# Attention, MoE and top-2 MoE on one core: the float64 weights are converted by VectorE alone, with an integer addition, under a new hand-written order

## The chip, the cores and the metric

The kernel runs on one core of a Trainium2 chip. A core has TensorE (PE, matrix products, with PEld for its weight loads), VectorE (DVE), ScalarE (ACT), GpSimd (POOL) and SyncE (SP, which issues most DMA transfers here). Each engine takes its own queue in order, and semaphores make one wait for another. The metric is the device time of the whole program in microseconds. Runs of this kernel differ by about 0.5% (1080.51 to 1086.46 us).

## The reference

```python
# q, k, v, f_logit: (4, 8, 768, 48) float32
f = 1 / (1 + exp(-f_logit))
for t in range(768):                      # decaying linear attention, state per head 48 x 48
    state = f[t][:, None] * state + outer(k[t], v[t])
    y[t] = q[t] @ state
x = y as (3072 tokens, 384)
x = relu(x @ w_in) ** 2 @ w_out           # 384 -> 2048 -> 384; w_in and w_out are float64
noisy = x @ w_gate + log1p(exp(x @ w_noise)) * noise       # 8 experts, the two largest per token
out = sum over the two: share * (relu(x @ w1[e]) @ w2[e])  # 384 -> 1024 -> 384
```

## The kernel before

**Stages.** Attention works in 24 chunks of 128 tokens, all 8 heads at once. Chunk by chunk there are preparation steps (f, k and q transposed and multiplied by products of decays, which VectorE makes with two scans) and attention units (`a_A`, `a_k`, `a_U`, `a_Y` twice with `a_S`). Three chunks make a block of 384 tokens. The first MoE goes over 8 blocks and 16 slices of its inner width, 128 units in all: `mm1` (9 products), ScalarE's relu and square, VectorE's low part `gl`, and two units later `mm2` (9 products). Then come the choice of experts, the gathering of rows by GpSimd, and the second MoE.

**High and low parts.** TensorE's operands are pairs: a high part rounded to the engine's fast type and a low part, the rest. Three products (high by high, high by low, low by high) make one exact enough product. So every weight piece needs a high and a low part.

**The weights of the first MoE.** They come as float64 words in 16 pieces (`w_load`, alternately of `w_in` and `w_out`, each 128 partitions by 768 numbers of two 32-bit words). The first four have staging places of their own, the others share one place for each kind, so the load of a piece waits until the piece two before it has been read. `conv_a` builds the float32 number from the high word, with sign, exponent and 20 bits of the mantissa: on VectorE a shift (line 379), a step that sets the sign (line 380) and a mask that keeps the exponent (`cv_p`, line 382). ScalarE turns the low word into a float (line 387; VectorE does it for pieces 0, 12 and 14 with a product, line 385) and rounds the high part (line 390). GpSimd multiplies the low word's float by the exponent (line 392) and joins the two (line 393). `conv_b` subtracts the high part to get the low part (line 403): on GpSimd, and on VectorE for pieces 8 and 15 (`BY_DVE`).

**Other work on the same engines.** On VectorE: the scans (lines 472, 482), a limit on four numbers between them (line 474, `rF`), the masked products `AM` (515), the state (`S`, 532 and 533), the low parts of x (589), the square `g` for units 8 to 31 (625) and `gl` (628). On GpSimd: the products of q from chunk 6 on (494).

**The order.** Up to the end of the second pass over the weights (units 0 to 31) the order of the program is written out in a string, `ORDER`: W and E, V are loads, P preparation steps, a attention units, A and B the two halves of a conversion, x the low parts of attention's result, M units of the first MoE, L the opening of a pool. Each event appends its instructions to the engines' queues, SP's DMA queue among them. Behind it a loop issues unit after unit, with fixed offsets for all else.

Of the kernel before, what the change touches and what calls it, by code (L numbers as in the profile page):

```python
# [24 lines left out]
def general_path(tc, psum, dram, ident, wide, q, k, v, f_logit, w_in_v, w_out_v, w_gate, w_noise, noise, w1, w2, out,  # L25
                 rt):
    """The same function for any input, token after token, then tile after tile over all experts."""
# [150 lines left out]
def kernel(  # L178
# [52 lines left out]
    # ---------------------------------------------------------------- pools of the first phase  # L231
# [9 lines left out]
    # ---------------------------------------------------------------- constants  # L241
# [40 lines left out]
    # what the scans over the decays of all pairs add: they start anew in the columns between two pairs  # L282
# [24 lines left out]
    # ---------------------------------------------------------------- weights of the first MoE  # L307
# [23 lines left out]
    def w_load(i):  # L331
        """Rows of w_in come in the order of the rows of x^T."""
        kind, p = ("in", "out")[i % 2], i // 2
        n = 256 * WORDS
        shape = [128, 3, n] if kind == "in" else [128, 2, DM * WORDS]
        if i < RING:
            st = wpool.tile(shape, WDT, tag="w", name="st_first")
        else:
            st = LP["p"].tile(shape, WDT, tag=f"st_{kind}", name=f"st_{kind}", bufs=1)
        if kind == "in":  # L340
            for (r0, m, row0, rs) in ((0, 48, 0, 96), (64, 48, 48, 96), (48, 16, 288, 16), (112, 16, 336, 16)):
                s = bass.AP(tensor=w_in_v.tensor, offset=w_in_v.offset + row0 * DFF * WORDS + p * n,
                            ap=[[DFF * WORDS, m], [rs * DFF * WORDS, 3], [1, n]])
                nc.sync.dma_start(st[r0:r0 + m], s)
        else:
            nc.sync.dma_start(st, w_out_v[p * 256:p * 256 + 256, :].rearrange("(a p) d -> p a d", p=128))
        stage[i] = st

    CV = {}

    def w_parts(i):
        """The places of a piece in the tiles of high and low parts."""
# [9 lines left out]
        # columns in the order that the 32x32 transposes of r_store undo  # L362
# [7 lines left out]
    def conv_a(i):  # L370
        """float64 words to the nearest float32: the high word holds sign, exponent and 20 bits of
        the mantissa, the low word the rest. Signs and exponents come out right for magnitudes in
        [2**-126, 2); others raise the flag."""
        st = stage.pop(i)
        if wide:
            src = st.rearrange("p a (f w) -> p (a f) w", w=2)
            lo_w, hi_w = src[:, :, 0], src[:, :, 1]
            a = LP["p"].tile([128, 768], I32, tag="cv_a", name="cv_a", bufs=2)
            nc.vector.tensor_scalar(a, hi_w, 0x08000000, 3, op0=OP.bitwise_xor, op1=OP.logical_shift_left)
            nc.vector.scalar_tensor_tensor(a, hi_w, -2147483648, a, op0=OP.bitwise_and, op1=OP.bitwise_xor)  # L380
            e = LP["p"].tile([128, 768], I32, tag="cv_p", name="cv_p", bufs=1)
            nc.vector.tensor_scalar(e, a, -8388608, None, op0=OP.bitwise_and)
            x = mp.tile([128, 768], F32, tag=f"x2{'ab'[i % 2]}", name="cv_x", bufs=1)
            if i in (0, 12, 14):
                nc.vector.scalar_tensor_tensor(x, lo_w.bitcast(U32), -2.0 ** -52, e.bitcast(F32), op0=OP.mult, op1=OP.mult)
            else:
                nc.scalar.activation(x, lo_w.bitcast(U32), AF.Copy, scale=-2.0 ** -52)
            a_f = a.bitcast(F32)
            for h_, _, cut in w_parts(i):
                nc.scalar.activation(h_, cut(a_f), AF.Copy, scale=-1.0)  # L390
            if i not in (0, 12, 14):
                nc.gpsimd.tensor_tensor(x, x, e.bitcast(F32), op=OP.mult)
            nc.gpsimd.tensor_tensor(x, x, a_f, op=OP.subtract)
        else:
            x = st.rearrange("p a f -> p (a f)")
            for h_, _, cut in w_parts(i):
                nc.scalar.activation(h_, cut(x), AF.Copy)
        CV[i] = x

    def conv_b(i, eng):  # L400
        x = CV.pop(i)
        for h_, l_, cut in w_parts(i):
            eng.tensor_tensor(l_, cut(x), h_.bitcast(F32), op=OP.subtract)

    # ---------------------------------------------------------------- attention
# [99 lines left out]
    def a_A(c):  # L505
        # the two heads of a pair lie in different rows of the array and run at the same time
# [37 lines left out]
    def a_Y(c, h):  # L544
# [5 lines left out]
        for p in (2 * h, 2 * h + 1):  # L550
            for s in range(2):
                # 16 rows more than the head has: they make room for a part of the last pair.
                # Only a half's first product clears the bank: the others find their columns cleared
# [31 lines left out]
    def a_x(c):  # L585
# [5 lines left out]
        if i == BT - 1:  # L591
            # the last pair's rows go where the other pairs leave room
# [5 lines left out]
    # ---------------------------------------------------------------- first MoE  # L598
    GB, acc = {}, {}

    # the first block is cut in two around the second, which gives the conversion of the weights time
# [62 lines left out]
    # ---------------------------------------------------------------- routing  # L664
# [15 lines left out]
    def r_logits(j):  # L680
        """The three parts of the sum over the model's width side by side in the array's columns."""
# [15 lines left out]
    def exp_a(x, n, w, names):  # L697
        """exp(x) of values that are not above zero, as the quotient of two sigmoids."""
# [25 lines left out]
    def softplus_noise(lg, pos, en, ln, noi_, n):  # L724
        """The logits with noise times softplus(x) = max(x, 0) + log1p(exp(-|x|))."""
# [110 lines left out]
    # ---------------------------------------------------------------- second MoE  # L836
# [12 lines left out]
    def segments(name, src, n, ne):  # L849
        """Rows in quarters: 32 partitions take one quarter each of 32 tokens."""  # L850
# [28 lines left out]
    def whole(e, t):  # L879
        """The first tokens are in a hurry: whole rows, and the tensor engine transposes them."""  # L880
# [9 lines left out]
    def gather_T(e, t):  # L890
        """x^T in the order of rows of the first MoE's x2^T: 32x32 blocks of the quarters are transposed."""
# [47 lines left out]
    # the first two experts take turns, which gives the last tokens' choices time  # L939
# [28 lines left out]
    def emm2(U):  # L968
# [5 lines left out]
        if final(e, hf):  # L974
            # tile after tile: only the last one's rows are still to be added when the products end
# [13 lines left out]
        if flipped(e, hf):  # L989
            # y^T: no columns for slots that are not there  # L990
# [55 lines left out]
    # ---------------------------------------------------------------- is the fast path exact?  # L1046
# [27 lines left out]
    def judge(step):  # L1074
        """Out of the fast path's reach: a weight's magnitude, a decay over a chunk that is too
        small to be divided by, or more tokens of an expert than its share of slots."""
# [25 lines left out]
    # ---------------------------------------------------------------- program  # L1102
# [3 lines left out]
    # The order of events up to the end of the second pass over the weights of the first MoE: loads (W) and  # L1106
    # conversion (A, B) of weights, loads of rows (E, V), preparation (P) and products (a, x) of attention,
    # products with the weights (M)
    ORDER = """
    P0 P1 P2 E1 W0 V0 P3 V1 P4 P5 P6 P7 a0 a1 P8 E2 W1 A0 E3 B0 a2 P9 W2 W3 P10 V2 a3 E4 P11 a4 V3 P12  # L1110
    A1 x0 a5 P13 a6 a7 P14 B1 W4 P15 A2 W5 a8 P16 B2 a9 A3 a10 E5 x1 W6 P17 V4 P18 a11 B3 P19 a12 a13 A4
    P20 a14 V5 P21 x2 W7 P22 B4 W8 a15 P23 a16 A5 a17 P24 a18 P25 A6 a19 B5 V6 P26 a20 P27 P28 M0 a21 M1
    P29 a22 B6 P30 a23 A7 x3 a24 W9 A8 W10 P31 x4 a25 P32 a26 M2 a27 M3 V7 W11 B7 P33 a28 a29 A9 x5 B8
    W12 M4 A10 P34 W13 P35 B9 W14 a30 M5 M6 V8 B10 a31 P36 M7 A11 a32 W15 A12 M8 B11 M9 a33 P37 M10 A13
    M11 B12 M12 B13 A14 P38 M13 A15 L0 a34 B14 M14 P39 M15 P40 a35 M16 a36 M17 x6 a37 P41 a38 a39 B15
    P42 M18 M19 a40 M20 P43 a41 M21 P44 a42 V9 a43 a44 P45 M22 x7 M23 P46 x8 P47 a45 M24 M25 P48 V10 M26
    a46 M27 a47 P49 a48 M28 P50 M29 M30 M31 V11
    """
    # pieces whose second half DVE converts
    BY_DVE = (8, 15)  # L1120
    # loads of v and steps of preparation that are among them
# [109 lines left out]
    uE = (NBLK - 1) * NF + LAG - 1  # L1231
    at(uE + 6, snapshot)
# [5 lines left out]
    def expert(n, loads, splits, gathers, flips):  # L1238
        """When the weights of an expert are loaded and split, and its tokens gathered and transposed."""
# [23 lines left out]
    def open_late():  # L1263
        """Where the weights were converted is room for another block of x."""
# [15 lines left out]
    def first_block(u):  # L1280
# [8 lines left out]
        "W": w_load, "A": conv_a, "B": lambda i: conv_b(i, nc.vector if i in BY_DVE else nc.gpsimd),  # L1289
# [7 lines left out]
    for u in range(2 * NF, NU + NEU + LAG):  # L1297
        if u == (NBLK - 1) * NF:
            open_p2()
        # first product  # L1300
# [8 lines left out]
        # attention runs ahead  # L1309
# [3 lines left out]
        # second product  # L1313
# [13 lines left out]
    # ---------------------------------------------------------------- the general path  # L1327
# [33 lines left out]
```

## Time and profile before

| | |
|---|---|
| median of 3 runs | 1085.11 us (1080.51 to 1086.46) |
| span of the profiled execution, first to last instruction | 1078.5 us |
| what lies around the span in that execution | not in the trace |
| TensorE busy | 1008.9 us (94%) |
| VectorE busy | 648.9 us (60%) |
| ScalarE busy | 492.9 us (46%) |
| GpSimd busy | 471.3 us (44%) |

Busy is the time in which an engine works on an instruction. Registers, branches, semaphores and the issue of DMAs don't count. Matmuls are pipelined, so a busy TensorE is not one at its peak.

### The profile page before, as it was taken

To read this page: it belongs to the slowest core of one execution; us is meant where nothing else is said; L and a number is where in the kernel's file an instruction comes from. 1 tells how busy PE (TensorE), PEld (TensorE's weight loads), DVE (VectorE), ACT (ScalarE), POOL (GpSimd) and SP (SyncE) were. 2 spreads that over 40 slices of the span, in tenths; PEclk is the share of its full clock that TensorE was granted. 3 is DMA by queue.
4 is the path that set the end of the run, shared out by engine and by line. 5 is a ranking of instruction groups with operands and counts; after the bars stand their busy time and mean duration, and the time that the engine had idled before them with its cause. 6 is when DMAs were issued, how large, how long until landed. Compare 5 with 4: busy or idle time off the path is not lost. (4 is left out here: it accounts for less than half of the span.)

```text
span 1078.5 us, 17435 instructions
## 1 busy us (share of the span) xinstructions
PE 1008.9 (94%) x6381; PEld 929.8 (86%) x6381; DVE 648.9 (60%) x1298; ACT 492.9 (46%) x1024; POOL 471.3 (44%) x527
## 2 busy tenths in 40 slices
PE   6577789999999999999999898999999999999996
PEld 4456779999889899898999787999989899999996
DVE  7999988878778777685335673353443443434420
ACT  2334434465556555555656642353343444434321
POOL 3775661003200303113123547777575757575523
PEclk9688889999999999999999999999999999999999
DMA  9886535547573645441023625344443535363413
GB/s 178 169 151 142 120 89 143 150 107 166 131 190 102 166 113 116 130 106 48 1 65 97 143 64 100 57 115 99 100 104 80 105 80 125 69 141 66 100 20 48
DMA packets 144782, 115.80 MB, mean 107 GB/s; under 512 B 75888, under 2 KB 128112, under 8 KB 144688
## 3 DMA queue, kind: packets, MB, share of 16 engines
q1 hardware_dynamic: 127248, 90.94, 35.6%
q0 software_dynamic: 15488, 20.52, 11.7%
q10 hardware_dynamic: 1952, 3.15, 1.2%
q8 instruction: 52, 0.85, 0.3%
q14 instruction: 42, 0.34, 0.1%
HBM read 89.08 MB, written 23.11 MB: 104 GB/s over the span
## 5 line engine op out<-in xcount | busy, mean ns | idle before, releaser
L875 POOL DMA_INDIRECT gr<-x2s,seg x192 | 186.7, 972 | 74.4 <-issue 47.2
L615 PE MATMUL mm<-x,inh 128*128 128x384 f32 x768 | 203.2, 346 | 9.4 <-ACT r L618 9.4
L963 DVE SCALAR_TENSOR_TENSOR hl<-mm,hh 128x512 fp32r<-128x512 f32 (+1 forms) x120 | 71.6, 597 | 167.2 <-ACT hh L962 167.0
L615 PEld LDWEIGHTS mm<-x,inh 128*128 128x128 f32 x768 | 139.6, 192 | 14.0 <-ACT r L618 10.5
L628 DVE TENSOR_TENSOR gl<-g,gh 128x384 fp32r<-128x384 f32 x128 | 82.2, 646 | 106.1 <-ACT gh L623 85.6
L953 PE MATMUL mm<-gxh,eh 128*128 128x320 f32 (+1 forms) x384 | 138.1, 360 | 8.4 <-DVE hl L963 7.0
L1039 POOL DMA_INDIRECT out_dram<-y,tt x56 | 92.6, 1653 | 104.4 <-ACT y L1037 93.8
L648 PE MATMUL a<-gh,outh 128*128 128x384 f32 x384 | 136.5, 355 | 0.2
L953 PE MATMUL mm<-gxl,eh 128*128 128x320 f32 (+1 forms) x384 | 136.2, 355 | 0.4 <-DVE gxl L909 0.4
L953 PE MATMUL mm<-gxh,el 128*128 128x320 f32 (+1 forms) x384 | 135.9, 354 | 0.0
L962 ACT ACTIVATE hh<-mm 128x512 fp32r<-128x512 f32 (+1 forms) x120 | 62.4, 520 | 154.3 <-PE mm L953 153.8
L648 PE MATMUL a<-gl,outh 128*128 128x384 f32 x384 | 130.2, 339 | 1.5 <-DVE gl L628 1.5
L615 PE MATMUL mm<-x,inl 128*128 128x384 f32 x384 | 131.0, 341 | 0.0
L648 PE MATMUL a<-gh,outl 128*128 128x384 f32 x384 | 130.0, 338 | 0.0
L494 POOL TENSOR_TENSOR qT<-qT,F 128x512 f32<-128x512 f32 x18 | 24.5, 1361 | 228.9 <-DVE qT L418 179.9
L618 ACT ACTIVATE r<-mm 128x384 f32<-128x384 f32 x128 | 62.0, 484 | 81.1 <-PE mm L615 79.5
L953 PEld LDWEIGHTS mm<-gxh,eh 128*128 128x128 f32 x384 | 72.5, 189 | 16.2 <-DVE hl L963 8.7
L318 DVE TENSOR_TENSOR el<-est,eh 128x512 fp32r<-128x512 f32 x96 | 64.5, 686 | 36.1 <-ACT eh L315 35.8
L953 PEld LDWEIGHTS mm<-gxh,el 128*128 128x128 f32 x384 | 72.6, 189 | 8.8
L953 PEld LDWEIGHTS mm<-gxl,eh 128*128 128x128 f32 x384 | 72.6, 189 | 6.7 <-DVE gxl L909 0.7
L648 PEld LDWEIGHTS a<-gh,outh 128*128 128x128 f32 x384 | 73.0, 190 | 5.9 <-issue 2.6
L648 PEld LDWEIGHTS a<-gl,outh 128*128 128x128 f32 x384 | 73.1, 190 | 2.3 <-DVE gl L628 2.2
(242 smaller groups left out, 2180.3 us busy)
## 6 DMA issues: line engine op xcount, KB each, us to landing
est<-in_moe_w_dram SPq DMA_DIRECT2D x56, 192.0 KB, 4.4
est<-in_moe_w_dram SPq DMA_DIRECT2D x14, 768.0 KB, 5.6
ck<-in_moe_w_in_dram SPq DMA_DIRECT2D x8, 768.0 KB, 5.2
ck<-in_moe_w_out_dram SPq DMA_DIRECT2D x8, 768.0 KB, 5.1
out_dram<-zeros SPq DMA_DIRECT2D x46, 128.0 KB, 3.4
v<-in_v_dram SPq DMA_DIRECT2D x24, 192.0 KB, 5.1
st_out<-in_moe_w_out_dram SPq DMA_DIRECT2D x6, 768.0 KB, 5.1
x2s<-x2q SPq DMA_DIRECT2D x32, 144.0 KB, 2.5
```

What stands on the lines that cost most here:

```text
L318: nc.vector.tensor_sub(lo, x, hi.bitcast(F32))
L494: eng.tensor_tensor(qT[c], PT.pop((c, "q")) if c < EARLY else qT[c], F, op=OP.mult)
L615: nc.tensor.matmul(ph, a[:, c, fs], b_[:, c, :], start=(n == 0), stop=(n == 8))
L618: nc.scalar.activation(r, ph, AF.Relu)
L628: nc.vector.tensor_sub(gl, g, gh.bitcast(F32))
L648: nc.tensor.matmul(acc[j][d], a[:, f % 4, ds_], b_, start=(first and n == 0), stop=(last and n == 2))
L875: nc.gpsimd.indirect_dma_start(out=g[:, b, :], out_offset=None, in_=src, in_offset=bass.IndirectOffsetOnAxis(ap=idx, axis=0))
L953: nc.tensor.matmul(ph[:, :n], a[:, c, fs], b_[:, c, o:o + n], start=(i == 0), stop=(i == 8))
L962: nc.scalar.activation(hh[:, :n], ph[:, :n], AF.Relu)
L963: nc.vector.scalar_tensor_tensor(hl[:, :n], ph[:, :n], 0.0, hh[:, :n].bitcast(F32), op0=OP.max, op1=OP.subtract)
L1039: st = nc.gpsimd.indirect_dma_start(out=out, out_offset=bass.IndirectOffsetOnAxis(ap=slots(e, T)[:m, 0:1].bitcast(I32), axis=0), in_=y[:m] ...
```

## The change

`conv_a` no longer splits off the exponent and no longer uses GpSimd. ScalarE scales the unsigned low word by 2^-29 and writes it as an integer, a number from 0 to 8: the three bits that the shift leaves empty, rounded. VectorE makes the high word with its sign, as before with another constant, and adds the integer to the number's bits. ScalarE does this for all 16 pieces. The high part becomes an event of its own, H (`conv_h`). `conv_b` always runs on VectorE. `a` lies in the ring places that `cv_x` had, and `cv_u` takes the place of `cv_a` and `cv_p` in the conversion's pool.

The order of the first phase is new. It has the same events otherwise: 16 loads and conversions, 51 preparation steps, 49 attention units, 9 events x, 32 units M. One more thing moves: `snapshot`, a copy of the experts' counts, from unit `uE + 6` to `uE + 1` near the end of the first MoE, while `uE` itself has the same value. Everything else in the diff is comments.

```diff
         if wide:
             src = st.rearrange("p a (f w) -> p (a f) w", w=2)
             lo_w, hi_w = src[:, :, 0], src[:, :, 1]
-            a = LP["p"].tile([128, 768], I32, tag="cv_a", name="cv_a", bufs=2)
-            nc.vector.tensor_scalar(a, hi_w, 0x08000000, 3, op0=OP.bitwise_xor, op1=OP.logical_shift_left)
+            u = LP["p"].tile([128, 768], I32, tag="cv_u", name="cv_u", bufs=2)
+            nc.scalar.activation(u, lo_w.bitcast(U32), AF.Copy, scale=2.0 ** -29)
+            a = mp.tile([128, 768], I32, tag=f"x2{'ab'[i % 2]}", name="cv_a", bufs=1)
+            nc.vector.tensor_scalar(a, hi_w, 0x18000000, 3, op0=OP.bitwise_xor, op1=OP.logical_shift_left)
             nc.vector.scalar_tensor_tensor(a, hi_w, -2147483648, a, op0=OP.bitwise_and, op1=OP.bitwise_xor)
-            e = LP["p"].tile([128, 768], I32, tag="cv_p", name="cv_p", bufs=1)
-            nc.vector.tensor_scalar(e, a, -8388608, None, op0=OP.bitwise_and)
-            x = mp.tile([128, 768], F32, tag=f"x2{'ab'[i % 2]}", name="cv_x", bufs=1)
-            if i in (0, 12, 14):
-                nc.vector.scalar_tensor_tensor(x, lo_w.bitcast(U32), -2.0 ** -52, e.bitcast(F32), op0=OP.mult, op1=OP.mult)
-            else:
-                nc.scalar.activation(x, lo_w.bitcast(U32), AF.Copy, scale=-2.0 ** -52)
-            a_f = a.bitcast(F32)
-            for h_, _, cut in w_parts(i):
-                nc.scalar.activation(h_, cut(a_f), AF.Copy, scale=-1.0)
-            if i not in (0, 12, 14):
-                nc.gpsimd.tensor_tensor(x, x, e.bitcast(F32), op=OP.mult)
-            nc.gpsimd.tensor_tensor(x, x, a_f, op=OP.subtract)
+            nc.vector.tensor_tensor(a, a, u, op=OP.add)
+            CV[i] = a.bitcast(F32)
...
-    def conv_b(i, eng):
+    def conv_h(i):
+        for h_, _, cut in w_parts(i):
+            nc.scalar.activation(h_, cut(CV[i]), AF.Copy)
+
+    def conv_b(i):
         x = CV.pop(i)
         for h_, l_, cut in w_parts(i):
-            eng.tensor_tensor(l_, cut(x), h_.bitcast(F32), op=OP.subtract)
+            nc.vector.tensor_tensor(l_, cut(x), h_.bitcast(F32), op=OP.subtract)
...
     ORDER = """
-    P0 P1 P2 E1 W0 V0 P3 V1 P4 P5 P6 P7 a0 a1 P8 E2 W1 A0 E3 B0 a2 P9 W2 W3 P10 V2 a3 E4 P11 a4 V3 P12
-    A1 x0 a5 P13 a6 a7 P14 B1 W4 P15 A2 W5 a8 P16 B2 a9 A3 a10 E5 x1 W6 P17 V4 P18 a11 B3 P19 a12 a13 A4
-    P20 a14 V5 P21 x2 W7 P22 B4 W8 a15 P23 a16 A5 a17 P24 a18 P25 A6 a19 B5 V6 P26 a20 P27 P28 M0 a21 M1
...
+    E1 P0 P1 P2 P3 a0 P4 P5 P6 V0 W0 a1 A0 E2 P7 W1 A1 H0 W2 E3 P8 V1 a2 a3 a4 V2 W3 P9 x0 B0 P10 W4
+    H1 A2 a5 P11 W5 P12 a6 B1 P13 H2 P14 E4 a7 a8 P15 B2 a9 a10 x1 a11 A3 V3 P16 a12 W6 P17 a13 P18
+    a14 A4 E5 P19 V4 H3 P20 x2 a15 P21 W7 a16 H4 B3 P22 B4 W8 P23 P24 A5 P25 V5 a17 A6 H5 a18 P26 P27
+    P28 H6 a19 B5 a20 M0 x3 M1 A7 V6 M2 B6 A8 a21 H7 a22 P29 a23 a24 B7 P30 W9 a25 x4 W10 P31 P32 a26
+    P33 a27 H8 M3 P34 a28 A9 a29 W11 B8 x5 M4 V7 W12 W13 A10 M5 H9 H10 P35 a30 V8 a31 B9 M6 A11 M7 B10
+    a32 a33 W14 H11 M8 W15 M9 A12 P36 M10 H12 B11 A13 P37 M11 H13 B12 M12 B13 M13 M14 A14 A15 H14 L0
+    P38 a34 a35 M15 M16 P39 M17 P40 a36 M18 P41 a37 B14 x6 a38 a39 M19 a40 V9 x7 H15 B15 P42 a41 P43
+    M20 P44 M21 V10 a42 a43 P45 a44 M22 x8 M23 V11 M24 P46 P47 a45 M25 M26 P48 P49 M27 M28 a46 M29 P50
+    M30 a47 a48 M31
     """
-    BY_DVE = (8, 15)
...
-    uE = (NBLK - 1) * NF + LAG - 1
-    at(uE + 6, snapshot)
+    uE = (NBLK - 1) * NF + 1
+    at(uE + 1, snapshot)
...
-        "W": w_load, "A": conv_a, "B": lambda i: conv_b(i, nc.vector if i in BY_DVE else nc.gpsimd),
+        "W": w_load, "A": conv_a, "H": conv_h, "B": conv_b,
```

## Rows read from the trace of the kernel before

**Rows 1.** The page: busy time, share, instructions; TensorE's busy tenths in 40 slices.

```profile
PE 1008.9 (94%) x6381; PEld 929.8 (86%) x6381; DVE 648.9 (60%) x1298; ACT 492.9 (46%) x1024; POOL 471.3 (44%) x527
...
PE   6577789999999999999999898999999999999996
```

**Rows 2.** Busy time by stage: PE, PEld, DVE, ACT, POOL, clock, DMA, GB/s.

```profile
0.00:66.00 66.00, 40.41 (x310) 30.94 (x312) 58.11 (x75) 21.85 (x43) 38.46 (x58) 0.84 1.01 169
66.00:160.00 94.00, 71.80 (x436) 65.79 (x434) 86.72 (x93) 41.84 (x84) 59.41 (x36) 0.85 0.60 125
160.00:1078.00 918.00, 896.64 (x5647) 833.10 (x5643) 504.02 (x1132) 429.25 (x897) 373.47 (x435) 1.00 0.44 101
```

**Rows 3.** Waits from 0 to 160 us: in total, times, longest.

```profile
PE t L526 <- ACT cv_x L387: 9.2, 1, 9.2
...
PE t L554 <- DVE AM L515: 7.1, 1, 7.1
...
ACT y L583 <- PE t L558: 4.5, 1, 4.5
```

**Rows 4.** Busy time in two short stretches, columns as in rows 2.

```profile
6.00:12.00 6.00, 5.27 (x23) 3.46 (x23) 5.62 (x9) 1.01 (x3) 0.00 (x0) 1.00 1.30 180
12.00:18.00 6.00, 3.68 (x36) 2.92 (x32) 5.79 (x9) 1.10 (x2) 0.00 (x0) 1.00 1.39 165
```

**Rows 5.** VectorE's timeline there: start, duration in us, line, operation.

```profile
6.00 1.26 DVE L472 TENSOR_TENSOR_SCAN F<-fT,anew 128x528 f32<-128x528 f32 x1 [4.01 <-ACT fT L442]
7.29 0.17 DVE L474 TENSOR_SCALAR rF<-F 128x4 f32<-128x4 f32 x1
...
7.71 1.25 DVE L482 TENSOR_TENSOR_SCAN G<-fT,anew 128x524 f32<-128x524 f32 x1
...
15.92 0.55 DVE L379 TENSOR_SCALAR cv_a<-st_first 128x768 int32<-128x768 int32 x1
16.50 0.96 DVE L380 SCALAR_TENSOR_TENSOR cv_a<-st_first,cv_a 128x768 int32<-128x768 int32 x1
...
18.09 0.96 DVE L385 SCALAR_TENSOR_TENSOR cv_x<-st_first,cv_p 128x768 f32<-128x768 uint32 x1
```

**Rows 6.** VectorE's groups, 0 to 160 us: busy, mean ns, idle before.

```profile
L628 DVE TENSOR_TENSOR gl<-g,gh 128x384 fp32r<-128x384 f32 x15 | 19.5, 1314 | 1.5 <-ACT gh L623 0.6
L472 DVE TENSOR_TENSOR_SCAN F<-fT,anew 128x528 f32<-128x528 f32 x8 | 11.7, 1466 | 5.0 <-ACT fT L442 4.8
L482 DVE TENSOR_TENSOR_SCAN G<-fT,anew 128x524 f32<-128x524 f32 x8 | 11.4, 1422 | 0.1
L474 DVE TENSOR_SCALAR rF<-F 128x4 f32<-128x4 f32 x8 | 10.3, 1293 | 0.3
L382 DVE TENSOR_SCALAR cv_p<-cv_a 128x768 int32<-128x768 int32 x16 | 9.6, 598 | 1.4
...
L625 DVE TENSOR_TENSOR g<-r 128x384 f32<-128x384 f32 x7 | 6.4, 910 | 4.0 <-ACT r L618 3.9
...
L533 DVE TENSOR_TENSOR S<-S,FE 128x192 f32<-128x192 f32 x4 | 3.9, 979 | 0.1
```

**Rows 7.** The same groups' shortest, median and longest ns, 0 to 160 us.

```profile
L533 DVE TENSOR_TENSOR S<-S,FE x4: 357/840/1879, 31.2 to 79.8; 128x192 f32<-128x192 f32 x4
L625 DVE TENSOR_TENSOR g<-r x7: 530/557/2009, 129.6 to 158.4; 128x384 f32<-128x384 f32 x7
L628 DVE TENSOR_TENSOR gl<-g,gh x15: 549/1147/2204, 76.5 to 159.1; 128x384 fp32r<-128x384 f32 x15
```

**Rows 8.** Line 379 (shift) alone: VectorE busy, clock, DMA, GB/s.

```profile
0.00:160.00 160.00, 16.58 (x16) 0.85 0.76 143
```

**Rows 9.** Line 380 (sign step) alone, columns as in rows 8.

```profile
0.00:160.00 160.00, 22.15 (x16) 0.85 0.76 143
```

**Rows 10.** Line 403 (low parts) alone: VectorE busy, GpSimd busy, clock, DMA, GB/s.

```profile
0.00:160.00 160.00, 2.22 (x1) 30.63 (x20) 0.85 0.76 143
```

**Rows 11.** A group of ScalarE, 0 to 160 us: busy, mean ns, idle before.

```profile
L387 ACT ACTIVATE cv_x<-st_in 128x768 f32<-128x768 uint32 x4 | 3.6, 904 | 1.1 <-DVE inl L403 1.0
```

More of the change, by code (lines that the diff above doesn't have):

```diff
@@ L377, in conv_a @@
             lo_w, hi_w = src[:, :, 0], src[:, :, 1]
-            a = LP["p"].tile([128, 768], I32, tag="cv_a", name="cv_a", bufs=2)
-            nc.vector.tensor_scalar(a, hi_w, 0x08000000, 3, op0=OP.bitwise_xor, op1=OP.logical_shift_left)
+            u = LP["p"].tile([128, 768], I32, tag="cv_u", name="cv_u", bufs=2)
+            nc.scalar.activation(u, lo_w.bitcast(U32), AF.Copy, scale=2.0 ** -29)
+            a = mp.tile([128, 768], I32, tag=f"x2{'ab'[i % 2]}", name="cv_a", bufs=1)
+            nc.vector.tensor_scalar(a, hi_w, 0x18000000, 3, op0=OP.bitwise_xor, op1=OP.logical_shift_left)
             nc.vector.scalar_tensor_tensor(a, hi_w, -2147483648, a, op0=OP.bitwise_and, op1=OP.bitwise_xor)
-            e = LP["p"].tile([128, 768], I32, tag="cv_p", name="cv_p", bufs=1)
-            nc.vector.tensor_scalar(e, a, -8388608, None, op0=OP.bitwise_and)
-            x = mp.tile([128, 768], F32, tag=f"x2{'ab'[i % 2]}", name="cv_x", bufs=1)
-            if i in (0, 12, 14):
-                nc.vector.scalar_tensor_tensor(x, lo_w.bitcast(U32), -2.0 ** -52, e.bitcast(F32), op0=OP.mult, op1=OP.mult)
-            else:
-                nc.scalar.activation(x, lo_w.bitcast(U32), AF.Copy, scale=-2.0 ** -52)
-            a_f = a.bitcast(F32)
-            for h_, _, cut in w_parts(i):
-                nc.scalar.activation(h_, cut(a_f), AF.Copy, scale=-1.0)
-            if i not in (0, 12, 14):
-                nc.gpsimd.tensor_tensor(x, x, e.bitcast(F32), op=OP.mult)
-            nc.gpsimd.tensor_tensor(x, x, a_f, op=OP.subtract)
-        else:
[L395 to L398, printed above, removed]
-    def conv_b(i, eng):
+            nc.vector.tensor_tensor(a, a, u, op=OP.add)
+            CV[i] = a.bitcast(F32)
+        else:
+            CV[i] = st.rearrange("p a f -> p (a f)")
+    def conv_h(i):
+        for h_, _, cut in w_parts(i):
+            nc.scalar.activation(h_, cut(CV[i]), AF.Copy)
+    def conv_b(i):
         x = CV.pop(i)
         for h_, l_, cut in w_parts(i):
-            eng.tensor_tensor(l_, cut(x), h_.bitcast(F32), op=OP.subtract)
+            nc.vector.tensor_tensor(l_, cut(x), h_.bitcast(F32), op=OP.subtract)
     qT, kT, KT, AM, X = {}, {}, {}, {}, {}
@@ L1109 @@
     ORDER = """
-    P0 P1 P2 E1 W0 V0 P3 V1 P4 P5 P6 P7 a0 a1 P8 E2 W1 A0 E3 B0 a2 P9 W2 W3 P10 V2 a3 E4 P11 a4 V3 P12
-    A1 x0 a5 P13 a6 a7 P14 B1 W4 P15 A2 W5 a8 P16 B2 a9 A3 a10 E5 x1 W6 P17 V4 P18 a11 B3 P19 a12 a13 A4
-    P20 a14 V5 P21 x2 W7 P22 B4 W8 a15 P23 a16 A5 a17 P24 a18 P25 A6 a19 B5 V6 P26 a20 P27 P28 M0 a21 M1
[L1113 to L1117, printed above, removed]
+    E1 P0 P1 P2 P3 a0 P4 P5 P6 V0 W0 a1 A0 E2 P7 W1 A1 H0 W2 E3 P8 V1 a2 a3 a4 V2 W3 P9 x0 B0 P10 W4
[7 more added lines that the diff above has]
+    M30 a47 a48 M31
     """
-    BY_DVE = (8, 15)
     PLANNED = tuple(sum(e[0] == k_ for e in ORDER.split()) for k_ in "VP")
```

## The prediction

> **What bounds the kernel now.** The page comes first. Over the whole span TensorE is busy 94% of the time and VectorE 60% [rows 1], and from the digits of the 40 slices the reader is to see where that average is not true: TensorE stands at 5 to 8 in the first six slices and at 9 nearly everywhere behind them. So I cut the span where TensorE's idling ends. The busy times by stage [rows 2] show it in numbers. From 160 us on TensorE is busy 896.6 of 918 us at a granted clock of 1.00, the 2.4 GHz level: 21 us idle in the whole rest. From 0 to 160 us it is busy 40.4 + 71.8 = 112.2 us, so 48 us idle, at a granted share of 0.84 and 0.85, which is time at the 1.2 GHz level mixed in. In the same 160 us VectorE is busy 58.1 + 86.7 = 144.8 us, 90.5%. Nearly all of the weight conversion lies there: of its shifts and sign steps all 16 [rows 8, 9], of its low parts on GpSimd and VectorE 21 instructions [rows 10]. The longest waits [rows 3] say the same: TensorE waited 7.1 us for a masked product of VectorE, and 9.2 us for a ScalarE instruction in line behind a conversion. The first 160 us go at VectorE's pace, the other 918 at TensorE's.
>
> Next I asked why VectorE is that busy, and compared one instruction with itself. From 6 to 18 us GpSimd does nothing (0.00 us busy) while the DMA engines are at their fullest (share 1.30 and 1.39) [rows 4], and VectorE's instructions take there [rows 5]: the shift 0.55 us, the sign step 0.96, the limit on four numbers 0.17, the scans 1.26 and 1.25. Over the 160 us the same limit takes 1.29 us in the mean, the low part `gl` 1.31 [rows 6] against a shortest one of 0.549 [rows 7]. VectorE is stretched where GpSimd works, and not where the DMA queues are full.
>
> **The change, part by part** (VectorE, 0 to 160 us; first what goes).
> - Stretching, each group's busy time less its count times its unstretched duration: `gl` 19.5 - 15 x 0.549 = 11.3; the limit 10.3 - 8 x 0.17 = 8.9; scans 11.7 - 8 x 1.26 = 1.6 and 11.4 - 8 x 1.25 = 1.4; `g` 6.4 - 7 x 0.53 = 2.7; `S` 3.9 - 4 x 0.357 = 2.5 [rows 5 to 7]; shift 16.58 - 16 x 0.55 = 7.8 [rows 8]; sign step 22.15 - 16 x 0.96 = 6.8 [rows 9]. Sum 43.0 us. The kernel after has no conversion on GpSimd, which was busy 38.5 + 59.4 us in this stretch [rows 2]. GpSimd keeps the products of q from chunk 6 on, two or so here, so a little stretching stays; I let that pass.
> - The exponent's mask: 9.6 us [rows 6], gone. The three products that VectorE made: 3 x 0.96 = 2.9 [rows 5], gone. Its one low part of weights, 2.2 [rows 10], is counted anew below. Together 14.7 us.
> - Added, the integer addition, 16 times. The trace has none. The nearest row is the sign step, the same 128x768 integers with two inputs and one output: 0.96 us, 15.4 in all, and that is my value. Bounds: below, the shift with one input, 0.55 (8.8 in all); above, the scan per element, 1.26 x 768/528 = 1.8 (29 in all).
> - Added, the low parts of pieces 0 to 13: seven of 128x768 at 0.96, seven of two halves of 128x384 at 0.549 each [rows 7]: 6.7 + 7.7 = 14.4. Bounds: two 0.549 for each 768 (one us more in all), or 2.2 each if they were stretched as the one row of today [rows 10].
> - ScalarE: three more conversions of the low word at 0.90 us [rows 11], 2.7 us, now written as integers. ScalarE is busy 21.9 + 41.8 of 160 us, so this hides; uncovered it costs those 2.7. The high parts are the same copies, under an event of their own.
> - The snapshot of the counts moves to a place beyond 160 us under TensorE's full stretch, one short instruction: nothing. The order's other events are the same set, moved. Loads too: each weight piece still waits for its ring place, so a late conversion holds the loads of v and of rows queued behind it on SP, before and after alike.
>
> Net: -43.0 - 14.7 + 15.4 + 14.4 = -27.9. VectorE's work up to the point that is now at 160 us falls from 144.8 to 117 us. With the addition's bounds it is 110 to 131.
>
> Another reading of the stretching would be the DMA traffic into the same memory. Then the 43.0 us would stay, and the sum would be -14.7 + 29.8 = +15 instead of -28. Against it stands the shift at 0.55 us at a DMA share of 1.39 with GpSimd idle [rows 4, 5]; I give it no chance of its own. The Trainium skill, "SBUF — State Buffer", section "Who interferes with whom", decides the same way: VectorE and GpSimd share one pair of ports, which one of them holds for a whole instruction, and a DMA never contends with an engine. By that rule the sum is the -28.
>
> **From work to time.** VectorE was 90.5% busy. With 117 us of work it stands close to TensorE, which has 112 us at the clock of today, an estimated 95 at the full clock (112.2 x 0.85). Two queues in order that hand work to each other, with nearly the same load, leave more holes than one that always lags. I take 85%: 117 / 0.85 = 138 us instead of 160, 22 us less. At 92% it is 127 (-33), at 78% it is 150 (-10). Behind this point TensorE has its 918 us as before, so what is gained here is kept.
>
> The profiled span is 1078.5 us; the trace has nothing of what lies around it, and the median of the runs is 1085.11, 6.6 above. I carry the difference over: 1085.1 - 22 = 1063 us.
>
> **Rivals.**
> 1. New waits eat the gain (slower). The addition waits for ScalarE's low word, and ScalarE takes its queue in order: right behind `a14`, for instance, it first does the high parts of attention, which wait for TensorE. Such a wait was 4.5 us long once [rows 3]. Behind the waiting addition stand the next scans and masks, and TensorE waits for those. VectorE does 0.55 + 0.96 us of its own before the addition, ScalarE needs 0.90. If half of the 16 pieces met a 4.5 us hold: +36 us, 1063 + 36 = 1099. It decides from 22/16 = 1.4 us a piece. For it: the 9.2 us that TensorE was held behind ScalarE. Against: ScalarE is idle 96 of 160 us, and VectorE, at 90.5%, can have waited 15 us at most in today's order, which hands it ScalarE's results too.
> 2. The loads set the first part. From 0 to 66 us the DMA share is 1.01 at 169 GB/s [rows 2], so weights and rows may come no sooner, and only the second part gains. By GpSimd's busy time 61% of the relief is there, 17 us: (86.7 - 17)/0.85 = 82 instead of 94, -12, 1073. For: that share, and the new string asks for piece 1 (A1) beside P7 of the second chunk, where before it came with P12 of the third, so VectorE may stand before a load that SP has queued behind E1, V0, W0 and E2. Against: VectorE was late there, not idle: 58.1 of 66 us.
> 3. Hidden anyway: VectorE's relief lies under TensorE's work. If the 48 us of TensorE's idling before 160 us come from hand-overs of one engine to the other and not from VectorE's load, nothing changes: 1085. For: TensorE's 94% of the span against VectorE's 60% [rows 1]. Against: the same 160 us with VectorE at 90.5% and the first two waits of [rows 3]. The Trainium skill, "Perfetto Trace Analysis", section "Identifying the Most-Contended Engine", speaks for this rival: the engine with the highest occupancy is the one to work on first, which here is TensorE. Its section "Optimization Strategy" adds that a kernel can have stages with different engines, and the rows of the stages bear that out.
> 4. More than forecast: VectorE stays 95% busy, as a queue that lags does: 117/0.95 = 123, -37, 1048.
>
> **How the numbers follow.** Forecast (1052 to 1075) 0.62; rival 2 0.12; rival 4 0.11; rival 3 0.08; rival 1 0.07. A measurement of this kernel can tell about 0.5%, 5.4 us, from no change. Faster: 0.62 + 0.12 + 0.11 = 0.85; same 0.08; slower 0.07. The range reaches from a part of rival 4 to the near edge of rival 3: 1050 to 1080. The addition's upper bound (+13.6/0.85 = 16 us, 1079) lies inside.
>
> **What would show it.** Right: the limit on four numbers near 0.17 us and `gl` near 0.55 in the mean up to the end of the first phase, the addition near 0.96, no conversion on GpSimd, TensorE's unbroken full-clock stretch beginning near 138 us, and a stretch of about 918 us behind it. Wrong: a VectorE instruction waiting for ScalarE's low word, on many pieces, by more than 1.4 us; a limit that still takes over 1 us; an addition of 1.8 us or more; or a first low conversion idle until its load has landed. If the full stretch begins 22 us earlier and the end does not, the last step is the wrong one.

## The result, and the profile after

| | before | after |
|---|---|---|
| median, 4 runs each | 1084.47 us (1080.51 to 1086.46) | 1053.60 us (1049.63 to 1055.94) |
| span of the profiled execution | 1078.5 us | 1053.8 us |
| unit 0 of the first MoE begins | 66.7 us | 65.3 us |
| unit 16 begins (the second pass over the weights) | 160.0 us | 132.1 us |
| unit 64 begins | 356.4 us | 327.5 us |
| first product of the second MoE | 606.5 us | 580.4 us |

The ratio is 0.9721, 95% interval 0.9690 to 0.9753: 30.9 us faster by the medians, 24.7 us from span to span. The forecast was 1063 us. The profiled execution of after took 1055.57 us with a span of 1053.8, so 1.8 us lie around the span. The starts in the table are cut 0.2 to 0.3 us ahead of the first product's own row in the timeline (65.59 and 132.31 us after, 66.91 and 160.29 before), which changes no difference by more than 0.1 us.

The page first: busy time, share and instructions, then tenths of the 40 slices.

```profile
PE 997.5 (95%) x6381; PEld 924.4 (88%) x6381; DVE 620.8 (59%) x1316; ACT 495.2 (47%) x1027; POOL 378.9 (36%) x477
...
PE   4779999999999999999998998999999999999996
```

GpSimd worked 92 us less than in [rows 1] and VectorE 28 us less, with 18 instructions more. TensorE's line now reaches 9 in the fourth slice, where it took seven. Then the windows, cut where units 0 and 16 begin (columns as in rows 2).

```profile
0.00:65.30 65.30, 39.68 (x318) 32.85 (x320) 53.19 (x87) 23.05 (x46) 5.06 (x40) 0.79 1.03 173
65.30:132.10 66.80, 59.25 (x429) 56.05 (x426) 62.34 (x96) 40.15 (x79) 3.45 (x5) 1.00 0.83 168
132.10:1053.00 920.90, 898.52 (x5642) 835.54 (x5640) 505.32 (x1134) 431.95 (x903) 370.41 (x432) 0.99 0.45 101
```

Against [rows 2]: the first stage is hardly shorter, the second 66.8 us instead of 94 (cut there 0.7 us ahead of unit 0), the rest 921 instead of 918. In the first two stages VectorE has 53.2 + 62.3 = 115.5 us of work where it had 144.8, and GpSimd 8.5 us where it had 97.9. TensorE is busy 98.9 us instead of 112.2, with the same work, because its clock is 1.00 through the whole second stage; and it is idle 33.2 us instead of 47.8. So on TensorE's account the 27.9 us come in two nearly equal parts, 13.3 of clock and 14.6 of idling. This says where TensorE saved the time, and not what caused it: no run changed the clock by itself.

VectorE's groups from 0 to 132.1 us (busy, mean ns, idle before):

```profile
L384 DVE CUSTOM_DVE_ANT_0 cv_a<-cv_a,cv_u 128x1536 uint16<-128x1536 uint16 x15 | 14.4, 959 | 2.1 <-ACT cv_u L380 0.2
L475 DVE TENSOR_TENSOR_SCAN G<-fT,anew 128x524 f32<-128x524 f32 x8 | 10.0, 1246 | 0.1
L465 DVE TENSOR_TENSOR_SCAN F<-fT,anew 128x528 f32<-128x528 f32 x8 | 9.9, 1236 | 4.4 <-ACT fT L435 4.4
L621 DVE TENSOR_TENSOR gl<-g,gh 128x384 fp32r<-128x384 f32 x15 | 9.1, 609 | 0.9
L396 DVE TENSOR_TENSOR outl<-cv_a,outh 128x384 fp32r<-128x384 f32 x14 | 7.1, 550 | 0.0
L396 DVE TENSOR_TENSOR inl<-cv_a,inh 128x768 fp32r<-128x768 f32 x7 | 6.6, 949 | 0.0
...
L618 DVE TENSOR_TENSOR g<-r 128x384 f32<-128x384 f32 x7 | 3.8, 548 | 0.6 <-ACT r L611 0.5
...
L526 DVE TENSOR_TENSOR S<-S,FE 128x192 f32<-128x192 f32 x4 | 1.4, 357 | 0.1
...
L467 DVE TENSOR_SCALAR rF<-F 128x4 f32<-128x4 f32 x8 | 1.4, 170 | 0.3
```

Beside [rows 6], every kind that was there before has fallen to its shortest time or near it: the limit from 1293 to 170 ns, `S` from 979 to 357, `gl` from 1314 to 609. The first line is the addition; the profile shows it on pairs of 16-bit numbers, 959 ns each, and 15 of the 16 lie ahead of unit 16. Its column "idle before" says how long VectorE stood still for the low word: 0.2 us in all.

### The profile page after: what moved, and what is told of

Same layout as the page of the kernel before. It is cut to its first block, busy times and chain, and to the rows that moved or that the text cites. A ratio compares the mean times of both kernels' runs of the same rounds, so it can differ in the third digit from the quotient of the medians.

```text
span 1053.8 us, 17373 instructions
## 1 busy us (share of the span) xinstructions
PE 997.5 (95%) x6381; PEld 924.4 (88%) x6381; DVE 620.8 (59%) x1316; ACT 495.2 (47%) x1027; POOL 378.9 (36%) x477
## 5 line engine op out<-in xcount | busy, mean ns | idle before, releaser
L608 PE MATMUL mm<-x,inh 128*128 128x384 f32 x768 | 199.4, 340 | 1.9 <-DMA x<-y 1.0
L608 PEld LDWEIGHTS mm<-x,inh 128*128 128x128 f32 x768 | 137.1, 188 | 6.2 <-issue 4.5
L621 DVE TENSOR_TENSOR gl<-g,gh 128x384 fp32r<-128x384 f32 x128 | 73.7, 578 | 107.0 <-ACT gh L616 97.6
L611 ACT ACTIVATE r<-mm 128x384 f32<-128x384 f32 x128 | 62.1, 485 | 84.6 <-PE mm L608 78.0
```

The lines of the kernel that those rows point to most:

```text
L608: nc.tensor.matmul(ph, a[:, c, fs], b_[:, c, :], start=(n == 0), stop=(n == 8))
L611: nc.scalar.activation(r, ph, AF.Relu)
L621: nc.vector.tensor_sub(gl, g, gh.bitcast(F32))
```

## The experiments

All of them ran on other chips of the same kind. There every kernel, the one before too, takes some 80 us more. In the traces from there nearly all of it lies in the second MoE (see the last section), while the first MoE agrees with the first chip. So each is told as its difference to the kernel before on the same chip, and by the stages up to unit 16. The changed kernel itself was run twice more, as `after_again` and `after_third`.

> The kernel after itself, for its time beside the kernel before on the chip of the next three runs. Every theory: 27 to 33 us under the kernel before.

> The kernel after itself once more, for its time on the chip of the next two runs: 26 to 31 us under the kernel before.

| run | minus before, us | ratio (95%) | unit 0 / unit 16 begins, us | first product of the second MoE, us |
|---|---|---|---|---|
| after_again | -26.0 | 0.9796 (0.9748 to 0.9843) | 66.5 / 131.8 | 577.7 |
| after_third | -32.5 | 0.9718 (0.9676 to 0.9760) | 64.2 / 130.9 | 576.8 |
| e1, old order | -18.8 | 0.9849 (0.9809 to 0.9888) | 62.1 / 139.3 | 585.3 |
| e2, old conversion | +3.8 | 1.0042 (1.0013 to 1.0071) | 70.5 / 161.0 | 612.2 |
| e3, GpSimd reads for nobody | +22.7 | 1.0202 (1.0158 to 1.0247) | 73.1 / 176.2 | 632.2 |
| e4, rows loaded first | -31.9 | 0.9725 (0.9691 to 0.9759) | 61.3 / 131.4 | 578.0 |
| e5, addition twice | -9.1 | 0.9931 (0.9908 to 0.9954) | 68.6 / 145.6 | 597.4 |
| e6, no addition | -35.8 | 0.9684 (0.9645 to 0.9723) | 62.2 / 122.1 | 566.3 |
| e7, low parts on GpSimd | -17.6 | 0.9835 (0.9782 to 0.9888) | 69.5 / 135.9 | 583.6 |
| e8, GpSimd writes for nobody | -9.5 | 0.9933 (0.9901 to 0.9965) | 67.9 / 152.8 | 602.0 |
| e9, squares on ScalarE | -31.2 | 0.9723 (0.9682 to 0.9765) | 60.5 / 133.6 | 581.4 |

The gains of `after_again` and `after_third` lie 1 and 1.5 us outside what was expected of them. In these traces it is anything from 543 to 566 us from the second MoE's first product to the end (472 and 473 on the first chip), so a few us between two medians say little. The last column is free of that; on the first chip its figure is 606.8 before and 580.7 after. The three profiles of the changed kernel agree in it within 4 us, and at unit 16 within 1.2.

**Conversion or order? e1 and e2.** e1 keeps the new conversion and takes the order of before, each H right behind its A. e2 keeps the new order and takes the conversion of before.

```diff
 # e1
-        "W": w_load, "A": conv_a, "H": conv_h, "B": conv_b,
+        "W": w_load, "A": lambda i: (conv_a(i), conv_h(i)), "B": conv_b,
...                                                   # and ORDER of before
 # e2, in conv_a: the mask e and the float x of before, then
+                nc.gpsimd.tensor_tensor(x, x, e.bitcast(F32), op=OP.mult)
+            nc.gpsimd.tensor_tensor(x, x, a.bitcast(F32), op=OP.subtract)
...
 # e2, in conv_b
-            nc.vector.tensor_tensor(l_, cut(x), h_.bitcast(F32), op=OP.subtract)
+            (nc.vector if i in (8, 15) else nc.gpsimd).tensor_tensor(l_, cut(x), h_.bitcast(F32), op=OP.subtract)
```

> The conversion of the kernel after under the order of the kernel before (a high part right behind its conversion, low parts where they were). Theory A, that VectorE is freed of GpSimd's stretching whatever the order: at least two thirds of the 31 us are kept, 1054 to 1064 us, the limit on four numbers at 0.17 us. Theory B, that the new order brings the gain: about 1084 us. Theory C, that GpSimd's slow chain from a loaded piece to its low part made the weights late: as A, since that chain is gone here too.

> The conversion of the kernel before, with GpSimd, under the new order (the high part of piece 15 stands with its conversion). A: the stretching is back, the limit over 1 us in the mean, 1075 to 1090 us. B: about 1054 us. C: as A in time.

The conversion alone is worth 18.8 us, 61% of the 30.9 and a little under the two thirds expected; the order alone costs 3.8. With the conversion in place the order adds 7 to 8 us at unit 16 (139.3 against 130.9 to 132.1) and 7 to 14 at the end, against the three runs of the changed kernel. The windows of e1 and then e2:

```profile
62.10:139.30 77.20, 64.41 (x426) 59.11 (x425) 66.05 (x99) 41.88 (x85) 3.49 (x5) 0.96 0.72 149
```

```profile
70.50:161.00 90.50, 68.67 (x427) 63.45 (x426) 81.36 (x90) 38.03 (x77) 54.84 (x34) 0.85 0.64 130
```

VectorE's work in this stage goes with GpSimd's column and not with the order: 66 us beside 3.5 us of GpSimd, 81 beside 55 (e2 has the old conversion's instructions, too). The limit's shortest, median and longest in e2 are those of a stretched kernel again:

```profile
L474 DVE TENSOR_SCALAR rF<-F x8: 170/1590/2026, 7.3 to 120.8; 128x4 f32<-128x4 f32 x8
```

**Is it GpSimd's reading? e3.** The changed kernel, and GpSimd makes products of about the size of those before that nobody uses, each behind the addition or the low part.

```diff
...
+            for _ in range(1 if i in (0, 12, 14) else 2):
+                nc.gpsimd.tensor_tensor(LP["z"], LP["z"], CV[i], op=OP.mult)
...
```

and in `conv_b` one more of 128x768, or two of 128x384, except for pieces 8, 14 and 15.

> The kernel after, and beside it GpSimd makes as many products of the same size on a tile of its own as it made in the kernel before (two for most conversions, one or two halves for a low part, none for the low parts of pieces 8, 14 and 15). Nothing of the result hangs on them. A: the limit is back above 1 us, VectorE is stretched by 25 to 45 us in the first phase, and the time rises by 12 to 25 us, to 1066 to 1079. B and C: no wait goes through GpSimd, so 1054 us.

This is 22.7 us slower than before, 49 to 55 slower than the changed kernel, where 12 to 25 had been expected. Windows up to unit 16, and groups of VectorE:

```profile
0.00:73.10 73.10, 38.49 (x319) 32.19 (x320) 58.86 (x78) 21.66 (x42) 38.08 (x57) 0.77 0.90 142
73.10:176.20 103.10, 71.21 (x427) 65.02 (x424) 95.58 (x103) 40.94 (x81) 58.20 (x34) 0.85 0.55 118
```

```profile
L384 DVE CUSTOM_DVE_ANT_0 cv_a<-cv_a,cv_u 128x1536 uint16<-128x1536 uint16 x15 | 14.4, 959 | 2.1
L630 DVE TENSOR_TENSOR gl<-g,gh 128x384 fp32r<-128x384 f32 x15 | 13.2, 882 | 0.9
L484 DVE TENSOR_TENSOR_SCAN G<-fT,anew 128x524 f32<-128x524 f32 x8 | 12.9, 1611 | 0.1
...
L476 DVE TENSOR_SCALAR rF<-F 128x4 f32<-128x4 f32 x8 | 8.8, 1095 | 0.3
...
L382 DVE TENSOR_SCALAR cv_a<-st_in 128x768 int32<-128x768 int32 x6 | 6.6, 1098 | 3.6 <-POOL zz L405 3.6
```

VectorE has the same instructions as in after and needs 58.9 + 95.6 = 154.4 us for them instead of 115.5: 38.9 us of stretching, from 96 us of GpSimd's work. The prediction had put 43.0 on 97.9 us. Unit 16 comes 44.1 us later than in after: 38.9 of it is this work, 5.2 more idling of VectorE. No result of the conversion goes through these products, as it did through those before. But GpSimd reads a piece's tile, so two shifts had to wait until it had done so, 7.5 us in all (the last line shows 3.6 of them). TensorE stood 3.5 us longer for tiles that GpSimd clears (7.7 instead of 4.2). That much is GpSimd's latency, the rival explanation; the 38.9 us are longer instructions. The addition isn't stretched: no product of GpSimd ran during any of the 15.

**Reading or any work? e8.** The products are replaced by writes of zeros, 66 behind the additions (until unit 16) and 39 behind the low parts, each lot set off by a copy on ScalarE.

```diff
...
+            nc.scalar.activation(LP["z"][:, 0:1], CV[i][:, 0:1], AF.Copy)
+            for _ in range(3 if i in (0, 12, 14) else 5):
+                nc.gpsimd.memset(LP["z"], 0.0)
...
```

> The kernel after, and beside it GpSimd fills a tile of its own, five or three times for a conversion and three times for a low part (a copy of one column by ScalarE holds each group to its place). GpSimd is busy about as long as in the kernel before, and writes without reading. If it is GpSimd's reading that stretches VectorE's instructions of two inputs, these stay as short as in the kernel after (gl near 0.55 to 0.60 us, the scans at 1.25), only the shift and the limit may be stretched, and the time rises by 0 to 10 us. If any busy GpSimd stretches VectorE, gl goes over 1 us and the time rises by 30 us or more, as in the run with products beside.

```profile
L484 DVE TENSOR_TENSOR_SCAN G<-fT,anew 128x524 f32<-128x524 f32 x8 | 10.0, 1247 | 0.1
...
L630 DVE TENSOR_TENSOR gl<-g,gh 128x384 fp32r<-128x384 f32 x12 | 6.7, 557 | 7.6 <-ACT gh L625 7.1
...
L382 DVE TENSOR_SCALAR cv_a<-st_in 128x768 int32<-128x768 int32 x5 | 4.3, 853 | 1.3 <-ACT zz L403 1.3
```

With GpSimd writing for some 80 us, scans and `gl` keep their short times. Instructions with one input are longer in the mean (the shift of one kind 853 instead of 555 ns, the limit 290 instead of 170); of those with two, one square `g` took 1.02 us, beside GpSimd's product of q, which reads. The time of this run says nothing of stretching, though. It rose 23 us over `after_third`, where 0 to 10 had been expected, while VectorE's work up to unit 16 rose by 2.3 us only (117.5 against 115.2). By the waits, ScalarE's copies stood in its queue, waiting for VectorE's addition or for GpSimd, and attention behind them; that this is the whole of the 23 us wasn't tried.

```profile
ACT zz L388 <- DVE cv_a L384: 16.9, 7, 3.4
...
PE t L528 <- ACT KT L505: 10.5, 1, 10.5
...
ACT zz L403 <- POOL zz L390: 9.3, 5, 2.5
```

The Trainium skill, "SBUF — State Buffer", section "Who interferes with whom", says that a two-input instruction of VectorE contends with a GpSimd instruction that reads, not with one that only writes. The 557 and 882 ns of `gl` beside writes and beside reads agree.

**Does VectorE's work set the pace? e5 and e6.** e5 makes the addition a second time into a tile that nobody reads. e6 leaves the addition and the low word out, so its weights have the high word's bits only.

```diff
 # e5
+            b = LP["p"].tile([128, 768], I32, tag="cv_b", name="cv_b", bufs=1)
+            nc.vector.tensor_tensor(b, a, u, op=OP.add)
 # e6
-            nc.scalar.activation(u, lo_w.bitcast(U32), AF.Copy, scale=2.0 ** -29)
...
-            nc.vector.tensor_tensor(a, a, u, op=OP.add)
```

> The kernel after with the integer addition made twice (once into a tile that nobody reads): 16 x 0.96 = 15.4 us more work for VectorE in the first phase and nothing else. If VectorE still sets the pace of the first phase, as its 96% between the first and the ninth unit says, the time rises by 12 to 18 us over the kernel after. If TensorE has become the bound there, by 0 to 5 us.

> The kernel after without the integer addition and without ScalarE's low word: the weights lose the bits of the low word, and the result differs a little. VectorE has 15.4 us less to do. If VectorE sets the pace alone, the time falls by 12 to 17 us. If TensorE is close behind, as its 85 to 91% after the first unit says, it falls by 3 to 9 us.

Against `after_again`, on the same chip: e5 is 16.9 us slower by the medians, and its unit 16 comes 13.8 us later for 13.5 us more of VectorE's work (128.8 against 115.3 us up to there). e6 is 9.8 us faster, 9.7 at unit 16, for 12.4 us less (102.9 us; ScalarE loses 13 us too). More costs its whole price, less gives back four fifths, between the two expectations of e6 (3 to 9 and 12 to 17). Since e6 relieves ScalarE too, it is e5 that singles VectorE out. Windows of e5 and of e6, second stage:

```profile
68.60:145.60 77.00, 64.91 (x429) 60.51 (x426) 72.29 (x109) 40.11 (x80) 3.46 (x5) 0.93 0.70 148
```

```profile
62.20:122.10 59.90, 58.58 (x427) 55.93 (x426) 55.30 (x90) 32.04 (x69) 3.89 (x5) 1.00 0.91 195
```

In e6 TensorE is busy 58.6 of 59.9 us: with VectorE lighter still, the stage could not get much shorter.

**Where do the low parts belong? e7.** They go back to GpSimd, except pieces 8 and 15, by the line of e2's `conv_b`.

> The kernel after, but the low parts of the weights are made by GpSimd again (VectorE those of pieces 8 and 15, as in the kernel before); the integer addition stays. VectorE loses 14 us of work and is stretched by some 30 us of GpSimd's busy time again. Theory A, that GpSimd's traffic stretches VectorE: the stretching takes back at least what the work gives, 0 to 15 us over the kernel after, and the limit on four numbers is stretched again. If only the amount of work on VectorE counts: 8 to 14 us under the kernel after.

8.4 us slower than `after_again`. Up to unit 16 some 12.8 of the low parts' 13.8 us leave VectorE, and yet its work falls by 1.8 us only (113.5 against 115.3). The rest came back as stretching:

```profile
L384 DVE CUSTOM_DVE_ANT_0 cv_a<-cv_a,cv_u 128x1536 uint16<-128x1536 uint16 x15 | 16.4, 1091 | 3.2 <-ACT cv_u L380 0.9 <-DVE cv_a L383 0.6
L621 DVE TENSOR_TENSOR gl<-g,gh 128x384 fp32r<-128x384 f32 x15 | 10.9, 724 | 1.3 <-DVE g L618 0.5
...
L383 DVE SCALAR_TENSOR_TENSOR cv_a<-st_in,cv_a 128x768 int32<-128x768 int32 x6 | 7.9, 1316 | 0.2
```

The timeline shows it one by one. Three additions that began while GpSimd was at a low part took 1.78, 1.53 and 1.54 us; one that began 0.04 us ahead of a low part took 0.96. The limit, which was expected to be stretched again, was so once in eight times (1.63 us), the one time that it began during a low part.

Why the kernel is 8 us slower with VectorE's work about the same, whether by GpSimd's later low parts or otherwise, wasn't tried.

**The first 65 us: e4.** In after, TensorE stood still there for a load of rows that the DMA queue had behind a weight piece:

```profile
PE a L433 <- DMA early_rows<-in_f_logit_dram: 4.9, 1, 4.9
...
ACT cv_u L380 <- DMA st_first<-in_moe_w_out_dram: 4.3, 1, 4.3
```

The DMA queue's own row shows the load's predecessor, which waited until VectorE had read the ring place:

```profile
SPq L344 <- DVE cv_a L383: 12.7, 3, 8.5
```

e4 moves that load of rows (E5) ahead of W6.

```diff
-    A3 V3 P16 a12 W6 P17 ... a14 A4 E5 P19
+    A3 V3 E5 P16 a12 W6 P17 ... a14 A4 P19
```

> The kernel after with one event moved: the load of the last early rows (E5) stands before the load of piece 6, which holds SP's queue until piece 4 has been read. If that load sets when the first unit can begin (TensorE waited 4.9 us for it), the first unit begins 3 to 5 us earlier than at 65.3 us and the time falls by 2 to 5 us, to 1049 to 1052. If VectorE's work sets it, no change: 1054 us.

Unit 0 comes at 61.3, 3 to 5 us earlier than in the three profiles of the changed kernel (64.2 to 66.5), but unit 4 at 84.4, where it is in after (84.5): given back within four units. The time is that of the changed kernel, so the 2 to 5 us hoped for did not come.

```profile
61.30:131.40 70.10, 59.99 (x429) 55.97 (x426) 65.87 (x102) 40.78 (x80) 3.46 (x5) 1.00 0.80 171
```

VectorE is busy 65.9 of 70.1 us (94%). It has the same work to do whenever TensorE starts.

**An attempt at a faster kernel: e9.** e4, and ScalarE makes the square of units 8 to 31 too (`if True:` for `if F < NF // 2 or F >= 2 * NF:`), since it is idle more than a third of the stage.

> An attempt at a better kernel: the rows of E5 loaded ahead of piece 6, and the square of units 8 to 31 made by ScalarE as in all other units, which takes 24 x 0.55 us from VectorE, 8 units of it before the seventeenth unit. If VectorE sets the pace there: that unit begins 4 to 6 us earlier than in the kernel after, and the time falls by as much. If the longer chain on ScalarE (square, then rounding) holds the low parts up: no gain, or some us lost.

No gain: 1.3 us more than `after_third` on the same chip, with overlapping intervals, and unit 16 at 133.6 instead of 130.9, where 4 to 6 us earlier had been hoped for. VectorE's work up to unit 16 falls by 3.6 us (111.6 against 115.2), and it gets a wait for ScalarE; so does TensorE.

```profile
DVE gl L621 <- ACT gh L616: 5.1, 4, 2.6
...
PE mm L608 <- ACT r L611: 3.9, 1, 3.9
```

No version that was run beats the changed kernel beyond its interval, other than e6, which leaves work out.

## Why the prediction was right, and where its sizes were off

**The bound and the stretching: right.** In the changed kernel VectorE paces the time up to unit 16 (e5, e6). That it did so before is read from [rows 2] and borne out by e2 and e3, where a stretched VectorE put unit 16 back to 161.0 and 176.2 us. GpSimd's reads made it slow (e3, e8; e2 agrees). 43.0 us of stretching were put down; giving about the same reads back to the changed kernel cost 38.9.

**The addition: right.** 0.96 us was taken from the sign step, 0.959 measured, far from the upper bound of 1.8.

**The low parts: right.** 13.8 us in all (14 pieces, 21 instructions) against 14.4.

**VectorE's work: right.** 115.5 us up to unit 16, with one of the 16 additions still to come; 117 foretold.

**From work to time: mis-sized.** The share was taken as 85% for the whole of it; measured, 115.5 / 132.1 = 87.5%, so 132 us instead of 138. The mean hides two stages that went two ways. Up to unit 0 VectorE fell from 88% to 81% (53.2 of 65.3 us), and the gain there was 1.4 us: rival 2's outcome. Its mechanism, late loads, is a part of it only: TensorE stood 4.9 us for rows (e4), VectorE 0.8 us for a weight piece but 3.4 us for TensorE, and with a lighter VectorE and ScalarE unit 0 did come sooner (62.2 in e6, 64.2 to 66.5 in the changed kernel). Behind it VectorE stayed at 93% (62.3 of 66.8), near rival 4's 95%. The prediction, in rival 2, put 61% of the relief, 17 us, into the second stage by GpSimd's busy time; in fact 24.4 of the 29.3 us by which VectorE's work fell lie there, 83%, and 4.9 in the first. The new order spends the first stage's relief on work brought forward: VectorE makes 87 instructions there instead of 75 [rows 2], six pairs of scans instead of five. The clock is the other thing that the step left without a term: TensorE at 1.00 took 13.3 us off its own busy time, close to the "estimated 95 at the full clock". It stands at 1.00 from 65 us on, and not only from 138, as the sign of being right had it. That this lets it follow VectorE so closely is argued and not shown.

**"What is gained here is kept": nearly.** The two kernels are 28.9 us apart at unit 64, 26.1 at the second MoE and 24.7 at the end. The first loss is at the change between the two. PE's timeline, after and then before:

```profile
567.57 0.55 PE L895 MATMUL t<-ident,gp 128*128 128x128 f32 x3 [3.28 <-ACT gp L880]
```

```profile
594.57 0.55 PE L902 MATMUL t<-ident,gp 128*128 128x128 f32 x3 [1.45 <-ACT gp L887]
```

TensorE waited 1.8 us longer for the first gathered rows, and the 6.1 us behind that ran at a granted clock of 0.80:

```profile
570.00:576.10 6.10, 6.10 (x31) 6.07 (x31) 3.09 (x6) 4.95 (x12) 0.00 (x0) 0.80 0.71 168
```

That is one execution. In the traces of `after_again` and `after_third` TensorE stood 0.8 and 1.3 us ahead of these rows, and the second MoE began 3 to 4 us sooner than here (last column of the table), so the delay doesn't come in every execution.

**The carry-over of 6.6 us: misread.** It was taken as what lies around the span. After has 1.8 us there. With as much for before its profiled execution took 1080.3 us, which fits its fastest run (1080.51): the 6.6 us were mostly the distance of the fastest run from the median. From span to span the forecast was -22 and the result -24.7. By the medians it is -30.9: the profiled execution of before was 4.2 us under its median and that of after 2.0 over its own, which makes up the other 6.2. The gain differs by as much from chip to chip (-26.0, -30.9, -32.5).

So the 9.4 us between 1063 and 1053.6 add up, but for rounding, as 5.9 (more gained at unit 16 than forecast) - 3.2 (lost behind it) + 6.2 (which executions were profiled, and that is luck) + 0.6 (between the two medians of before). The result lies at the fast edge of the forecast's band (1052 to 1075): the mechanism was right, the step from work to time too cautious.

**The rivals.** 1 (new waits for the low word) did not occur: 0.2 us in 15 additions. 2's outcome came in the first stage, its mechanism there in part: e4's row shows one late load, and freeing it gains nothing. 3 (hidden) is out by the result, and by e5. 4 nearly held for the second stage (93%), not for the whole.

## What to carry to other kernels

Compare an instruction with itself, where the neighbouring engine is idle and where it is busy: a limit on four numbers at 0.17 and at 1.29 us told more than the shares of busy time. Elementwise work given to GpSimd isn't free when VectorE paces the stage: in e7, taking 12.8 us of low parts off VectorE lowered its work by 1.8. And turn saved work into saved time stage by stage: here 1.4 us of the 27.9 came up to unit 0 and 26.5 behind it, as VectorE's work fell by 4.9 and 24.4 us.

## What the hardware showed that was not expected

The addition of 32-bit integers stands in the profile as one custom instruction on 128x1536 16-bit numbers, at 959 ns the price of any two-input instruction of that length here. Scans were stretched beside reading GpSimd work (1246 to 1611 ns in e3) and not beside its writes (1247 in e8), although they are one long dependent chain.

On the chips of the experiments the second MoE was some 80 us longer in every trace, and the changed kernel's own rows on such a chip (`after_third`) show ScalarE waiting there, where the profile of the first chip shows no such wait:

```profile
ACT hh L955 <- remote: 84.0, 15, 13.5
```

The profile names no releaser within the core; what it was stays open.
